# A third raw-weight buffer, loads in the order of use, and decoding and decay work moved, in a one-core state-space and expert kernel

## The chip, the cores and the metric

One core of one Trainium2 chip runs the whole program. The metric is the device time of one execution in microseconds (us); lower is better. Five engines work side by side, each through its own queue strictly in order: PE (TensorE, matrix products), ACT (ScalarE), DVE (VectorE), POOL (GpSimd) and SP, which here only issues transfers. An instruction whose operand or buffer is not ready holds up everything behind it on its engine.

## The reference

Three stages follow one another on 3072 tokens (4 sequences of 768) with 256 channels. Inputs are 32-bit floats; the three weights of stage two arrive as 64-bit floats.

```python
# stage 1: 8 heads, state 16 x 32, chunked along the sequence
cum = cumsum(log(a)); L = exp(cum[i] - cum[j]) for j <= i
y = (C B^T * L) x + (C state) * exp(cum)
state = exp(sum(log a)) * state + sum_j B_j x_j exp(cum_last - cum_j)
# stage 2
x = ((y @ w_a) * (y @ w_b)) @ w_out          # 256 -> 1536 -> 256
# stage 3: eight experts, the best of eight for each token
out[t] = gate * sigmoid * relu(x[t] @ w1[e]) @ w2[e]
```

## The kernel before, in words

**Tiles and stages.** The tokens are 24 tiles of 128, numbered `t`; tiles are prepared in units of two (`G = 2`). Stage two works on blocks of tiles (`BLK`, two tiles each for the first four blocks) and on 12 slices `f` of the 1536 inner columns (`NF1 = 12`). The code calls a slice's weights a unit as well; here they are "weights `f`". Every product of stage two is done as three float32r products of high and low halves (`mm3`, L513: `hi*hi`, `hi*lo`, `lo*hi`).

**One tile of stage one** (`attn_stages`): `tr` transposes B, Cq and cp on PE (`ptr`, L339) and ACT copies them out (`cd` L343, `BT` L345); `cb` multiplies them on PE (`pcb`, L365) and DVE multiplies by the decay mask (`mt`, L369); `ys` makes the output on PE (`py`, L386 to L396), ACT takes its high half (`xh`, L402), DVE its low half (`xl`, L403), and DVE updates the running state (`stm` L407, `Sst` L411). `pcb` of a tile needs the PSUM bank that `py` of the tile before used, so it waits for `xl` and `stm`. POOL prepares `cp`, `Cq`, `Bq` (L295) and the masks `lm` (L303) two tiles ahead (`prep`).

**Decays.** `decays(r)` computes the decay factors of half of all tiles (`r = 0` for tiles 0 to 11, `r = 1` for 12 to 23) in some 25 short DVE instructions (L213 to L252), eight PE transposes `pd` (L207), two or more ACT copies to `EX` (L208), one POOL product `dtmp` (L257) and one DVE sum `dec` (L264). The second group is queued when tile 7 is begun (`ahead(7)`), although tile 12 is the first to need it.

**Weights of stage two.** `load_w(f)` brings 768 KB of raw 64-bit weights into one of two `raw` buffers (`stg`, `bufs=2`; 256 KB each of `w_a`, `w_b`, `w_out`, L439 and L442). They are decoded to float32 halves in six pieces (`split_w`): ACT makes `u` (L464), DVE does `low3` (L468), `sign` (L472) and `join` (L476), ACT makes the high half `whi` (L480), DVE the low half `wlo` (L483). Weights 0 are decoded in three parts of 256 columns (`w_a`, `w_b`, `w_out`: lists `wa`, `wb`, `wo`), all others in one of 768. A raw buffer is free again after `sign`. `u` and `t` are work tiles of two buffers each.

**What sets the order.** The start of the program (tiles 0 and 1) is written out by hand, inside `tc.manual_schedule`, for PE, ACT, DVE and POOL. There the `wb` and `wo` parts and all of weights 1 (`w1_`) are decoded after tiles 0 and 1, in one run. From the barrier on, a scheduler orders the instructions, from a program in which `tick` after every product unit takes steps from three lists: attention steps (`pend`), background work (`bg`: `prep`, the second decays, loads of B and C) and decode pieces (`dq`, at `RATE`). SP issues the loads in program order.

Of the kernel before, what the change touches and what calls it, by code (L numbers as in the profile page):

```python
# [18 lines left out]
def kernel(  # L19
# [52 lines left out]
    stg = ctx.enter_context(tc.tile_pool(name="stg", bufs=2))  # L72
# [93 lines left out]
    def load_bc(u):  # L166

        v = wk.tile([P, 2, G, H, N], F32, tag="BCin", name="BCin")
        for j, src in ((1, B), (0, C)):
            for i in range(G):  # L170
                b, c = divmod(u * G + i, NCH)
                nc.sync.dma_start(
                    out=v[:, j, i], in_=src[b, :, c * P:(c + 1) * P, :].rearrange("h p n -> p h n"))
        BCin[u] = v
# [12 lines left out]
    rfs = cst.tile([NR, 2, P], F32, name="rfs")  # L187
# [5 lines left out]
    def decays(r):  # L193
# [5 lines left out]
        ar = araw[:, r, :]  # L199
        rf, rs = rfs[:, 0], rfs[:, 1]  # L200
        a0, T, A, Eb, t2, t3 = (small(n) for n in ("a0", "T", "A", "Eb", "t2", "t3"))
        bc = lambda t, n=SUB: t.unsqueeze(2).to_broadcast([NR, n, SP_])
# [37 lines left out]

        def ends():

            q = st["q"]
            V.tensor_copy(out=A, in_=a0)
            for i in range(SUB - 1):
                V.tensor_scalar(out=A[:, i + 1:], in0=A[:, i + 1:], scalar1=T[:, i:i + 1], scalar2=None, op0=ALU.mult)
            for i in range(1, SUB):
                V.tensor_scalar(out=Eb[:, 0:i], in0=Eb[:, 0:i], scalar1=T[:, i:i + 1], scalar2=None, op0=ALU.mult)
            V.tensor_tensor(out=sub(q[:, 1]), in0=sub(q[:, 0]), in1=bc(A), op=ALU.mult)
            V.tensor_tensor(out=sub(q[:, 2]), in0=sub(rs), in1=bc(Eb), op=ALU.mult)  # L250
            V.tensor_tensor(out=t3[:, 0:1], in0=T[:, 0:1], in1=Eb[:, 0:1], op=ALU.mult)
            V.tensor_copy(out=q[:, 3], in_=t3[:, 0:1].to_broadcast([NR, P]))  # L252
# [14 lines left out]
        return dict(new=new, factors=factors, pairs=pairs, ends=ends, tot=tot, tots=tots,  # L267
# [55 lines left out]
    def attn_stages(t):  # L323
# [51 lines left out]
        def ys(alt=False):  # L375
# [23 lines left out]
            if m not in xT:  # L399
# [45 lines left out]
    def split_w(f):  # L445
# [7 lines left out]
        def wide_pieces(s):  # L453
# [417 lines left out]
    def load_first2():  # L871
        for f0, n, tag in ((0, 3, "w64b"), (3, 3, "w64b"), (6, 2, "w64v")):
            r = wk.tile([P, n, DM], F32, tag=tag, name="raw2")
# [17 lines left out]
    with tc.manual_schedule(engines={ET.Activation, ET.DVE, ET.Pool, ET.PE}):  # L891
        load_a(0)
        load_bc(0)
        consts_early()
        load_x(0)
        load_w(0)
        load_x(1)
        load_bc(1)
        load_w(1)
        load_x(2)  # L900
        load_x(3)
        load_a(1)
# [4 lines left out]
        done = {"x": 4, "bc": 2}  # L907
# [4 lines left out]
        dq = []  # L912
        late_, first = [], []
        for f in range(NF1 + 1):
            ps = split_w(f) if f < NF1 else []
            if f < 2:
                first.append(ps)
                ps = []
            dq.extend(late_[:1] + ps[:1] + late_[1:])
            late_ = ps[1:]  # L920
            if f + 2 < NF1:
                late_.append(lambda f=f: load_w(f + 2))
# [8 lines left out]

        def ahead(t):
# [579 lines left out]
```

## Time and profile before

| | |
|---|---|
| median of three timed runs | 622.99 us (621.7 to 623.39) |
| the profiled execution | 621.96 us, of which span 620.3 us |
| PE busy | 569.3 us (92% of the span) |
| DVE busy | 325.5 us (52%) |
| ACT, POOL busy | 243.8 us (39%), 248.4 us (40%) |
| mean granted PE clock | 0.981 |

The span runs from the first to the last instruction of the profiled execution; its own time is 1.66 us longer. Busy time says how long an engine had an instruction in work, not that it was at its peak. The page of the profile cuts the span into 40 slices of 15.5 us and gives each engine's busy share in tenths. The other views list single instructions with their start, their duration and, in brackets, the idle time before them with the event that ended it. Matrix products overlap in the pipeline: the distance from one start to the next is what one of them costs.

### The profile page before, as it was taken

What the parts mean: (1) busy time and instruction counts of PE and PEld (TensorE: products, weight loads), DVE (VectorE), ACT (ScalarE), POOL (GpSimd) and SP (SyncE); (2) the same over time, 40 slices, a digit from 0 to 9 for tenths busy, and PEclk for the clock granted to TensorE, in tenths of its full rate; (3) what the DMA queues carried; (4) which work ended last, traced back from release to release, by engine and by line L of the source; (5) the groups of instructions that cost most, each with busy time, mean ns of one, the idle gap of its engine ahead of it and who ended that gap; (6) DMA issues with size and microseconds to landing.
All of it is one profiled execution on the core that took longest, in us unless ns stands there. A gap on an engine that the chain in (4) does not pass through costs nothing. (4 is left out here: it accounts for less than half of the span.)

```text
span 620.3 us, 11180 instructions
## 1 busy us (share of the span) xinstructions
PE 569.3 (92%) x4188; PEld 496.4 (80%) x4188; DVE 325.5 (52%) x894; ACT 243.8 (39%) x533; POOL 248.4 (40%) x319
## 2 busy tenths in 40 slices
PE   4369987999999999999999999999899999999991
PEld 2247867999897777777777889899788999999991
DVE  6779986224744434344232334544857556847620
ACT  3335553344333332332342233353345435445530
POOL 5547664333634433434222322364334433333111
PEclk9998997999999999999999999999999999999996
DMA  8597450002213210211000001221528345245000
GB/s 154 133 143 173 125 131 1 1 1 35 45 29 52 26 28 1 35 42 12 1 1 18 19 0 38 70 87 28 167 74 275 109 143 173 83 138 183 24 22 20
DMA packets 104920, 44.09 MB, mean 71 GB/s; under 512 B 81982, under 2 KB 99592, under 8 KB 104864
## 3 DMA queue, kind: packets, MB, share of 16 engines
q1 hardware_dynamic: 102128, 36.24, 23.7%
q0 software_dynamic: 2736, 7.12, 3.7%
q8 instruction: 34, 0.56, 0.4%
q14 instruction: 22, 0.18, 0.1%
HBM read 36.85 MB, written 6.95 MB: 71 GB/s over the span
## 5 line engine op out<-in xcount | busy, mean ns | idle before, releaser
L513 PE MATMUL pb<-xh,whi 128*128 128x256 f32 (+1 forms) x216 | 73.2, 339 | 1.7 <-ACT as__4671 L530 0.9
L513 PE MATMUL pa<-xh,whi 128*128 128x256 f32 (+1 forms) x216 | 72.0, 333 | 0.5 <-ACT xh L402 0.5
L513 PE MATMUL px<-gh,whi 128*128 128x256 f32 (+1 forms) x216 | 70.9, 328 | 0.0
L513 PE MATMUL pa<-xl,whi 128*128 128x256 f32 (+1 forms) x216 | 69.8, 323 | 0.0
L513 PE MATMUL px<-gl,whi 128*128 128x256 f32 (+1 forms) x216 | 69.2, 321 | 0.6 <-POOL gl L428 0.6
L513 PE MATMUL pa<-xh,wlo 128*128 128x256 f32 (+1 forms) x216 | 69.5, 322 | 0.0
L513 PE MATMUL px<-gh,wlo 128*128 128x256 f32 (+1 forms) x216 | 69.3, 321 | 0.0
L513 PE MATMUL pb<-xl,whi 128*128 128x256 f32 (+1 forms) x216 | 69.2, 320 | 0.0
L513 PE MATMUL pb<-xh,wlo 128*128 128x256 f32 (+1 forms) x216 | 69.1, 320 | 0.0
L1101 ACT ACTIVATE hh<-ph 128x384 fp32r<-128x384 f32 (+3 forms) x64 | 34.0, 531 | 69.7 <-PE ph L513 57.1
L1102 DVE SCALAR_TENSOR_TENSOR hl<-ph,hh 128x384 fp32r<-128x384 f32 (+3 forms) x64 | 38.7, 605 | 39.3 <-ACT hh L1101 33.8
L303 POOL TENSOR_SCALAR_AFFINE_SELECT lm<-EX 128x256 f32<-128x256 f32 x96 | 48.5, 541 | 24.2 <-DVE mt L369 22.6
L1121 PE MATMUL py<-eh,hh 128*128 128x256 f32 x200 | 57.0, 285 | 0.4 <-DVE hl L1102 0.4
L1121 PE MATMUL py<-el,hh 128*128 128x256 f32 x200 | 56.2, 281 | 0.0
L1121 PE MATMUL py<-eh,hl 128*128 128x256 f32 x200 | 56.1, 280 | 0.0
L1137 POOL DMA_INDIRECT out_dram<-yo,si x28 | 29.8, 1064 | 54.5 <-ACT yo L1134 47.7
L646 POOL DMA_INDIRECT xg<-x2d,gi x28 | 29.8, 1063 | 52.8 <-ACT lgx L661 36.9
L513 PEld LDWEIGHTS pb<-xh,whi 128*128 128x128 f32 x216 | 41.2, 191 | 10.7 <-issue 4.4
L513 PEld LDWEIGHTS pa<-xh,whi 128*128 128x128 f32 x216 | 41.3, 191 | 7.8 <-issue 3.7
L513 PEld LDWEIGHTS px<-gh,whi 128*128 128x128 f32 x216 | 41.0, 190 | 5.3 <-issue 2.1
L513 PEld LDWEIGHTS pa<-xh,wlo 128*128 128x128 f32 x216 | 41.4, 192 | 3.6 <-issue 0.3
L513 PEld LDWEIGHTS pa<-xl,whi 128*128 128x128 f32 x216 | 41.4, 192 | 3.3 <-issue 0.4
(685 smaller groups left out, 1402.3 us busy)
## 6 DMA issues: line engine op xcount, KB each, us to landing
raw<-in_moe_w_dram SPq DMA_DIRECT2D x30, 512.0 KB, 3.5
x2d<-xr SPq DMA_DIRECT2D x12, 272.0 KB, 2.2
xin<-in_x_dram SPq DMA_DIRECT2D x24, 128.0 KB, 2.9
raw<-in_moe_w_a_dram SPq DMA_DIRECT2D x12, 256.0 KB
raw<-in_moe_w_b_dram SPq DMA_DIRECT2D x12, 256.0 KB, 3.6
raw<-in_moe_w_out_dram SPq DMA_DIRECT2D x12, 256.0 KB, 4.1
BCin<-in_B_dram SPq DMA_DIRECT2D x26, 64.0 KB, 3.2
BCin<-in_C_dram SPq DMA_DIRECT2D x26, 64.0 KB, 3.1
```

Source lines behind the costliest of these rows:

```text
L303: nc.gpsimd.affine_select(out=Lm[t][:, :, s * SP_:(s + 1) * SP_], in_=exq(4 + s, b, c0 + i, 1).to_broadcast([P, H, SP_]), pattern=[[0, H], ...
L513: nc.tensor.matmul(out=out_, lhsT=l_, rhs=r_, start=first and i == 0, stop=last and i == 2, skip_group_check=skip)
L646: nc.gpsimd.indirect_dma_start(out=xg[:, q, :], out_offset=None, in_=x2d[0:nr, :], in_offset=bass.IndirectOffsetOnAxis(ap=sel["gi", i][:, ...
L1101: nc.scalar.activation(out=hh, in_=ph, func=AF.Relu)
L1102: V.scalar_tensor_tensor(out=hl, in0=ph, scalar=0.0, in1=hh.bitcast(F32), op0=ALU.max, op1=ALU.subtract)
L1121: nc.tensor.matmul(out=po, lhsT=l_[:, s_], rhs=r_, start=(f == 0 and j == 0 and q % 2 == 0), stop=(f == NF2 - 1 and j == 2), skip_group_ch ...
L1137: ins = nc.gpsimd.indirect_dma_start(out=out, out_offset=bass.IndirectOffsetOnAxis(ap=si[0:n_], axis=0), in_=yo, in_offset=None, bounds_ch ...
```

## The change

The raw weights get a third buffer (`stg`, `bufs=3`), and `load_w(2)` is issued at the start. The load of B and C is done tile by tile (`load_bc(u, i)`), and the first loads are issued in this order: B and C of tile 0, x of tile 0, B, C and x of tile 1, weights 0, weights 1, then B, C, x of tiles 2 and 3, weights 2. In the hand-written start four `wb` pieces stand before the `cb` of tile 1, the other two and the first `wo` piece before its `ys`. Weights 1 are no longer decoded in the start but stand in the list `dq` with the rest, and each further load follows its weights' pieces. The eight small products of `ends` (`A`, `Eb`, `all_`) become a step `parts`, which for the first group runs on POOL. The second group of decays is queued at tile 9, ahead of that tile's `prep`. `xl` comes after the state update. To make room, `u` of weights 0 to 5 uses the tiles `xr` and `x2T` in turn, `u` of weights 6 to 11 has one buffer in place of two, and `rfs` lies in the `cd` tiles.

```diff
-    stg = ctx.enter_context(tc.tile_pool(name="stg", bufs=2))
+    stg = ctx.enter_context(tc.tile_pool(name="stg", bufs=3))
...
+        def parts(g=None):
+            g = g or V
+            g.tensor_copy(out=A, in_=a0)
...
+            g.tensor_tensor(out=all_, in0=T[:, 0:1], in1=Eb[:, 0:1], op=ALU.mult)
...
             nc.scalar.activation(out=hi[:, :, i0:i0 + P], in_=py, func=AF.Copy)
-            nc.vector.tensor_tensor(out=lo[:, :, i0:i0 + P], in0=py,
-                                    in1=hi[:, :, i0:i0 + P].bitcast(F32), op=ALU.subtract)
             if c < NCH - 1:
...
+            nc.vector.tensor_tensor(out=lo[:, :, i0:i0 + P], in0=py,
+                                    in1=hi[:, :, i0:i0 + P].bitcast(F32), op=ALU.subtract)
...
-                    tl["u"] = wk.tile([P, 3 * DM], U32, tag="w64v", name="u", bufs=2)
+                    tag = ("xr", "x2T")[f % 2] if f < NE else "w64v"
+                    tl["u"] = wk.tile([P, 3 * DM], U32, tag=tag, name="u", bufs=1)
...
         load_a(0)
-        load_bc(0)
+        load_bc(0, 0)
         consts_early()
         load_x(0)
+        load_bc(0, 1)
+        load_x(1)
         load_w(0)
-        load_x(1)
-        load_bc(1)
         load_w(1)
+        load_bc(1, 0)
         load_x(2)
+        load_bc(1, 1)
         load_x(3)
+        load_w(2)
         load_a(1)
...
+        first = split_w(0)
+        dq = split_w(1) + [more_w]
...
-                if t == 7:
-
-                    d1 = decays(1)
-                    nop = lambda: None
-                    bg.extend([d1["new"], d1["factors"], d1["pairs"], d1["ends"], nop, nop, nop, nop,
-                               d1["ex"](0, 4), d1["ex"](4, 4), d1["tot"], d1["tots"]])
+                d1 = None
+                if t == 9:
+
+                    d1 = decays(1)
+                    bg.extend(d1[k_] for k_ in ("new", "factors", "pairs", "parts", "ends"))
...
         s0["tr"]()
+        dc["parts"](nc.gpsimd)
...
         dc["tot"]()
+        wb[0]()
+        wb[1]()
+        wb[2]()
+        wb[3]()
         s1["cb"]()
         s0["ys"](True)
         wa[5]()
+        wb[4]()
+        wb[5]()
+        wo[0]()
         dc["tots"]()
-        wb[0]()
         s1["ys"]()
-        for f_ in wb[1:] + wo:
+        for f_ in wo[1:]:
             f_()
         ahead(0)
         ahead(1)
-        bg.append(lambda: (load_bc(2), done.update(bc=3)))
-        bgstep()
-        for f_ in w1_:
-            f_()
-        bgstep()
-        dstep(2)
+        bg.append(more_bc)
+        bgstep(2)
         tc.no_sync_barrier()
```

How this moves instructions on two engines is shown at three places, in the order in which the built programs hold them. Line numbers differ by 3 to 4 between the two; the number behind a name is the buffer.

ACT, between the outputs of tile 1 (`xh`) and the copies of tile 2 (`cd`), before (`u_229` belongs to weights 0, `u_336` to weights 1, `u_407` to weights 2, `u_530` to weights 3):

```order
L402 ACTIVATE xh_289<-py_297 128x2x128
L480 ACTIVATE whi_107<-t_230 128x256
L464 ACTIVATE u_229<-raw_127 128x256
...
L464 ACTIVATE u_336<-raw_138 128x768
L480 ACTIVATE whi_107<-t_337 128x768
L464 ACTIVATE u_407<-raw_345 128x768
L530 ACTIVATE as__362<-pa_355 128x256
L464 ACTIVATE u_530<-raw_349 128x768
L343 ACTIVATE cd_389<-ptr_385,head2_81 128x128 x2
```

The same place in the changed program (`t_235` belongs to weights 0, `u_396` to weights 1, `u_544` to weights 2):

```order
L405 ACTIVATE xh_298<-py_308 128x2x128
L484 ACTIVATE whi_106<-t_235 128x256
L468 ACTIVATE u_396<-raw_132 128x768
L468 ACTIVATE u_544<-raw_145 128x768
L534 ACTIVATE as__351<-pa_344 128x256
L346 ACTIVATE cd_378<-ptr_374,head2_81 128x128 x2
```

Ahead of `cd` of tile 2 stood the rest of weights 0 (two `whi` and one `u`), all of ACT's part of weights 1, and `u` of weights 2 and 3. Now one `whi` of weights 0 stands there, and `u` of weights 1 and 2; `whi` of weights 1 and `u` of weights 3 come behind.

DVE, the last instructions ahead of the masks `mt` of tile 2, before (`t_337` is weights 1, `raw_345` and `t_408` weights 2, `raw_349` and `t_531` weights 3):

```order
L483 TENSOR_TENSOR wlo_108<-t_337,whi_107 128x768
L468 TENSOR_SCALAR raw_345<-raw_345 128x768
...
L472 SCALAR_TENSOR_TENSOR t_408<-raw_345 128x768
L468 TENSOR_SCALAR raw_349<-raw_349 128x768
L476 SCALAR_TENSOR_TENSOR t_408<-u_407,t_408 128x768
L472 SCALAR_TENSOR_TENSOR t_531<-raw_349 128x768
...
L483 TENSOR_TENSOR wlo_108<-t_408,whi_107 128x768
L369 TENSOR_TENSOR mt_396<-pcb2_398,lm_364 128x256
```

And in the changed program, from the output of tile 1 (`xl_299`) on (`raw_132` and `t_397` are weights 1, `raw_145` and `t_545` weights 2):

```order
L414 TENSOR_TENSOR xl_299<-py_308,xh_298 128x2x128
L472 TENSOR_SCALAR raw_128<-raw_128 128x256
L476 SCALAR_TENSOR_TENSOR t_235<-raw_128 128x256
L480 SCALAR_TENSOR_TENSOR t_235<-u_234,t_235 128x256
L487 TENSOR_TENSOR wlo_107<-t_235,whi_106 128x256
L472 TENSOR_SCALAR raw_132<-raw_132 128x768
L472 TENSOR_SCALAR raw_145<-raw_145 128x768
L476 SCALAR_TENSOR_TENSOR t_397<-raw_132 128x768
L476 SCALAR_TENSOR_TENSOR t_545<-raw_145 128x768
L480 SCALAR_TENSOR_TENSOR t_397<-u_396,t_397 128x768
```

Between tile 1's `xl` and tile 2's masks, which follow directly on this piece, there is now only the `w_out` part of weights 0, `low3` and `sign` of weights 1 and 2 and `join` of weights 1. Weights 1 and 2 were finished there before, and weights 3 begun; that work now stands behind the masks.

DVE around the updates of tile 7 (`xl`, `stm`), on which the second half of `pcb` of tile 8 waits, before:

```order
L540 TENSOR_TENSOR as__1050<-pb_1063,as__1050 128x256
L468 TENSOR_SCALAR raw_1414<-raw_1414 128x768
L483 TENSOR_TENSOR wlo_108<-t_1342,whi_107 128x768
L472 SCALAR_TENSOR_TENSOR t_1468<-raw_1414 128x768
L264 TENSOR_REDUCE dec_94<-dtmp_1115 128x12
L476 SCALAR_TENSOR_TENSOR t_1468<-u_1467,t_1468 128x768
L403 TENSOR_TENSOR xl_624<-py_1134,xh_623 128x2x128
```

The same place in the changed program:

```order
L472 TENSOR_SCALAR raw_1359<-raw_1359 128x768
L487 TENSOR_TENSOR wlo_107<-t_1287,whi_106 128x768
L544 TENSOR_TENSOR as__1045<-pb_1058,as__1045 128x256
L476 SCALAR_TENSOR_TENSOR t_1413<-raw_1359 128x768
L472 TENSOR_SCALAR raw_1464<-raw_1464 128x768
L408 TENSOR_TENSOR stm_1095<-py_1079,headh_80 128x128
L414 TENSOR_TENSOR xl_625<-py_1079,xh_624 128x2x128
```

The sum `dec` of the second decays is gone from here; it now stands behind the masks of tile 9. From the `pcb` of tile 8 on the order of PE is the same in both programs but for the eight `pd` transposes, which go from just ahead of tile 8's transposes to just ahead of tile 10's.

## Rows read from the trace of the kernel before

**Rows 1.** The page, span in 40 slices: PE busy, and PE's granted clock.

```profile
PE   4369987999999999999999999999899999999991
...
PEclk9998997999999999999999999999999999999996
```

**Rows 2.** Waits of PE: us in total, times, longest us.

```profile
PE pcb L365 <- ACT BT L345: 13.9, 3, 11.6
PE pcb L365 <- DVE stm L407: 4.6, 2, 3.8
```

**Rows 3.** Timeline of ACT, 20 to 35 us: start, duration, instruction [idle before].

```profile
23.03 0.42 ACT L480 ACTIVATE whi<-t 128x256 fp32r<-128x256 f32 x1 [2.71 <-DVE t L476]
...
30.18 0.37 ACT L530 ACTIVATE as__362<-pa 128x256 f32<-128x256 f32 x1
32.72 0.91 ACT L464 ACTIVATE u<-raw 128x768 f32<-128x768 f32 x1 [2.17 <-DMA raw<-in_moe_w_out_dram]
33.55 0.60 ACT L343 ACTIVATE cd<-ptr,head 128x128 f32<-128x128 f32 x2
```

**Rows 4.** Timeline of PE: the two long gaps, and products around 50 us.

```profile
34.48 1.24 PE L365 MATMUL pcb<-cd,BT 32*128 32x256 f32 x8 [11.56 <-ACT BT L345]
...
49.98 0.41 PE L513 MATMUL pa<-xl,whi 128*128 128x256 f32 x1
...
50.60 0.28 PE L513 MATMUL pb<-xh,wlo 128*128 128x256 f32 x1
...
96.19 1.22 PE L365 MATMUL pcb<-cd,BT 32*128 32x256 f32 x4 [3.84 <-DVE stm L407]
```

**Rows 5.** Timeline of POOL, 0 to 24 us.

```profile
1.88 0.20 POOL L132 TENSOR_TENSOR headh<-headm 128x4 f32<-128x4 f32 x1
2.16 0.19 POOL L134 TENSOR_TENSOR head<-headh 128x2 f32<-128x2 f32 x1
6.29 0.64 POOL L295 TENSOR_TENSOR cp<-BCin,EX 128x256 f32<-128x256 f32 x1 [3.94 <-DMA BCin<-in_C_dram]
8.59 4.02 POOL L303 TENSOR_SCALAR_AFFINE_SELECT lm<-EX 128x256 f32<-128x256 f32 x8 [1.65 <-ACT EX L208]
```

**Rows 6.** Timeline of SP, issue of the first x.

```profile
4.08 0.58 SPq L179 DMA_DIRECT2D xin<-in_x_dram  x1
```

**Rows 7.** Timeline of DVE, from tile 1's masks to tile 7's update.

```profile
15.61 1.35 DVE L369 TENSOR_TENSOR mt<-pcb,lm 128x256 f32<-128x256 f32 x3 [2.40 <-PE pyx L390]
...
21.55 0.53 DVE L468 TENSOR_SCALAR raw<-raw 128x256 uint32<-128x256 uint32 x1
...
36.06 1.35 DVE L369 TENSOR_TENSOR mt<-pcb,lm 128x256 f32<-128x256 f32 x3
...
51.39 0.42 DVE L540 TENSOR_TENSOR as__541<-pb,as__541 128x256 f32<-128x256 f32 x1
...
94.13 0.32 DVE L264 TENSOR_REDUCE dec<-dtmp 128x12 f32<-128x96 f32 x1 [2.94 <-POOL dtmp L257]
...
95.43 0.41 DVE L403 TENSOR_TENSOR xl<-py,xh 128x256 fp32r<-128x256 f32 x1
```

**Rows 8.** Busy time by stretch: PE, weight loads, DVE, ACT, POOL, granted clock, DMA.

```profile
51.39:95.43 44.04, 36.50 (x354) 31.34 (x353) 39.64 (x100) 24.50 (x58) 30.96 (x36) 0.99 0.55 132
...
101.50:445.00 343.50, 339.09 (x2504) 289.11 (x2503) 145.39 (x445) 126.60 (x297) 129.37 (x165) 1.00 0.15 33
...
50.37:96.19 45.82, 37.52 (x364) 32.26 (x362) 41.42 (x104) 25.97 (x60) 30.96 (x36) 0.98 0.55 130
96.19:101.50 5.31, 5.31 (x23) 4.66 (x24) 4.20 (x9) 0.61 (x2) 3.22 (x5) 0.50 0.00 0
```

**Rows 9.** Instructions touching tile q (second decays), 69 to 95 us: PE, weight loads, DVE.

```profile
69.00:95.00 26.00, 0.82 (x8) 0.75 (x8) 5.16 (x20) 0.99 0.43 105
```

**Rows 10.** Tile raw, 0 to 100 us: decode passes, ns min/median/max.

```profile
L468 DVE TENSOR_SCALAR raw<-raw x14: 281/552/811, 9.5 to 99.4; 128x768 uint32<-128x768 uint32 x11, 128x256 uint32<-128x256 uint32 x3
L472 DVE SCALAR_TENSOR_TENSOR t<-raw x13: 426/959/1500, 9.8 to 90.0; 128x768 uint32<-128x768 uint32 x10, 128x256 uint32<-128x256 uint32 x3
```

More of the change, by code (lines that the diff above doesn't have):

```diff
@@ L164, with load_bc @@
     xin, BCin = {}, {}
-    def load_bc(u):
-        v = wk.tile([P, 2, G, H, N], F32, tag="BCin", name="BCin")
+    def load_bc(u, i):
+        if i == 0:
+            BCin[u] = wk.tile([P, 2, G, H, N], F32, tag="BCin", name="BCin")
+        b, c = divmod(u * G + i, NCH)
         for j, src in ((1, B), (0, C)):
[L170 to L174, printed above, removed]
+            nc.sync.dma_start(out=BCin[u][:, j, i],
+                              in_=src[b, :, c * P:(c + 1) * P, :].rearrange("h p n -> p h n"))
     def load_x(t):
@@ L199, in decays @@
         ar = araw[:, r, :]
+        rfs = wk.tile([NR, 2, P], F32, tag="cd", name="rfs")
         rf, rs = rfs[:, 0], rfs[:, 1]
         a0, T, A, Eb, t2, t3 = (small(n) for n in ("a0", "T", "A", "Eb", "t2", "t3"))
+        all_ = cst.tile([NR, 1], F32, name=f"all{r}")
         bc = lambda t, n=SUB: t.unsqueeze(2).to_broadcast([NR, n, SP_])
@@ L239, in pairs @@
                                         scalar2=None, op0=ALU.mult)
+        def parts(g=None):
+            g = g or V
+            g.tensor_copy(out=A, in_=a0)
+            for i in range(SUB - 1):
+                g.tensor_scalar(out=A[:, i + 1:], in0=A[:, i + 1:], scalar1=T[:, i:i + 1], scalar2=None, op0=ALU.mult)
+            for i in range(1, SUB):
+                g.tensor_scalar(out=Eb[:, 0:i], in0=Eb[:, 0:i], scalar1=T[:, i:i + 1], scalar2=None, op0=ALU.mult)
+            g.tensor_tensor(out=all_, in0=T[:, 0:1], in1=Eb[:, 0:1], op=ALU.mult)
         def ends():
             q = st["q"]
[L244 to L248, printed above, removed]
             V.tensor_tensor(out=sub(q[:, 1]), in0=sub(q[:, 0]), in1=bc(A), op=ALU.mult)
             V.tensor_tensor(out=sub(q[:, 2]), in0=sub(rs), in1=bc(Eb), op=ALU.mult)
-            V.tensor_tensor(out=t3[:, 0:1], in0=T[:, 0:1], in1=Eb[:, 0:1], op=ALU.mult)
-            V.tensor_copy(out=q[:, 3], in_=t3[:, 0:1].to_broadcast([NR, P]))
+            V.tensor_copy(out=q[:, 3], in_=all_.to_broadcast([NR, P]))
         def tot():
@@ L265, in tots @@
                             in_=st["tmp"].rearrange("p b h c -> p b c h"), axis=AX.X, op=ALU.add)
-        return dict(new=new, factors=factors, pairs=pairs, ends=ends, tot=tot, tots=tots,
+        return dict(new=new, factors=factors, pairs=pairs, parts=parts, ends=ends, tot=tot, tots=tots,
                     ex=lambda k0, n: lambda: to_ex(k0, n))
@@ L872, in load_first2 @@
         for f0, n, tag in ((0, 3, "w64b"), (3, 3, "w64b"), (6, 2, "w64v")):
-            r = wk.tile([P, n, DM], F32, tag=tag, name="raw2")
+            r = wk.tile([P, n, DM], F32, tag=tag, name="raw2", bufs=1 if tag == "w64v" else None)
             nc.sync.dma_start(out=r, in_=w2[bass.ds(expert(0), 1), f0 * P:(f0 + n) * P, :]
@@ L906, with more_w @@
                                   in_=src[k * P:(k + 1) * P, :])
-        done = {"x": 4, "bc": 2}
+        done = {"x": 4, "bc": 2, "w": 3}
         bg = []
         RATE = [1.2, 0.6, 0.3, 0.4, 0.8]
-        dq = []
-        late_, first = [], []
-        for f in range(NF1 + 1):
+        def more_w():
+            if done["w"] < NF1:
+                load_w(done["w"])
+                done["w"] += 1
+        first = split_w(0)
+        dq = split_w(1) + [more_w]
+        late_ = []
+        for f in range(2, NF1 + 1):
             ps = split_w(f) if f < NF1 else []
-            if f < 2:
-                first.append(ps)
-                ps = []
             dq.extend(late_[:1] + ps[:1] + late_[1:])
-            late_ = ps[1:]
-            if f + 2 < NF1:
-                late_.append(lambda f=f: load_w(f + 2))
+            late_ = ps[1:] + [more_w]
         due = [0.0]
@@ L930, in dstep, with more_bc @@
                 due[0] -= 1
+        def more_bc():
+            for i in range(G):
+                load_bc(done["bc"], i)
+            done["bc"] += 1
         def ahead(t):
@@ L994 @@
         s0, s1 = st[0], st[1]
-        (wa, wb, wo), w1_ = first
+        wa, wb, wo = first
         V = nc.vector
```

5 lines of the change are left out of this document (3 added, 2 removed).

## The prediction

> **What bounds the kernel now.** I read the page's slices first. PE is at 9 tenths from the fourth slice to the last but one, except for a dip in the sixth and seventh; only the first seven slices, to about 108 us, leave it much idle, and there its clock dips too [rows 1]. So what this change can win lies before 108 us. From 101.5 to 445 us PE is busy 339.1 of 343.5 us [rows 8], and the order of instructions behind tile 8 is nearly the same: whatever PE gains by then is kept, whatever it loses is lost.
>
> The waits of PE name two large places, `pcb` on ACT's `BT` and `pcb` on DVE's `stm` [rows 2]; the timeline puts them at 34.48 us (11.56 us idle) and 96.19 us (3.84 us idle) [rows 4]. In the first, ACT tells why: `cd` of tile 2 stands behind the rest of weights 0, all of weights 1 and `u` of weights 2 and 3, and the last `u` waits 2.17 us for its raw weights to land [rows 3]. PE thus sits idle while decoding is done that its next products don't need. In the second, DVE waits 2.94 us for POOL's `dtmp` to make `dec`, with `xl` and `stm` queued behind it [rows 7]; no tile before 12 needs that sum.
>
> Two more things are to be seen. From 51.39 to 95.43 us DVE is busy 39.64 of 44.04 us against PE's 36.50 [rows 8]: there DVE, in its strict order, sets the pace. And PE runs at two levels: a product of 256 columns is listed with 0.41 us just before 50.2 us and 0.28 behind it [rows 4]; after the second gap the granted clock is 0.50 until 101.5 us [rows 8], 1.2 in place of 2.4 GHz.
>
> **The change, part by part.**
>
> *Loads and the first tile.* `cp` began at 6.29 us, on the landing of C [rows 5]. One more load, x of tile 0, now goes before that: at least its issue, 0.58 us [rows 6], at most about twice that if its transfer takes as long again. I take 0.8. The eight small products on POOL start every 0.28 us like two neighbours there [rows 5]: 2.2 us, into a hole of 1.65 us, the rest also within the 0.8. DVE is rid of them, but waits for POOL's result in the same hole: nothing. The swap of `xl` and the state update brings tile 1 forward by one `xl` at most, 0.41 us [rows 7]; I take half. Net, DVE is done with tile 1 at 21.6 us, as before (there `low3` began at 21.55 [rows 7]); bounds 21.2 to 22.4. The `wb` pieces now fill the 2.40 us in which DVE waited before tile 1's masks [rows 7] and the wait behind them: nothing, or some 2 us of DVE's time if that cover fails. B and C of tiles 2 and 3 now come behind weights 1 on SP's queue and land later by that transfer; the wait for ACT, until 26 us, covers POOL's work on them, and without it tile 2's transposes would wait for `Cq`.
>
> *The first gap.* For the `wo` part, `low3` to `whi` took 23.03 - 21.55 = 1.5 us, `whi` 0.42 [rows 3, 7]: ACT is at 23.5. Two `u` at 0.91, `as_` 0.37, then `cd` to `pcb`, 34.48 - 33.55 = 0.93 [rows 3, 4]: `pcb` at 26.6 us in place of 34.48, **7.9 us earlier**, if raw weights 2 have landed by 24.4; with the third buffer their load is issued without waiting for a release.
>
> *What is late next: DVE up to the product of slice 1 (51.39 us before [rows 7]).* From 21.6: `wo` 1.5 + 0.42 + 0.42; two `low3` at 0.55, two `sign` and one `join` at 0.96 (all passes of that size I take like `sign` [rows 10]) make 4.0: the masks of tile 2 start at 28.0 instead of 36.06 [rows 7]. Then come three masks of 1.35 us, two `wlo`, one `join` of weights 2, `sign` and `join` of weights 3 at 0.96, one `low3`, one product of 0.42, two tile updates (three instructions each, none over 0.41, so 1.0 together) and a constant: 4.05 + 4.8 + 0.55 + 0.42 + 2.0 + 0.2 = 12.0, so 40.0 without waits. I add 1.4 us, an estimate, for waits on `pcb`: 41.4 us, **10.0 us earlier**.
>
> *The DVE stretch, 51.39 to tile 7's `xl` (95.43).* Busy 39.64 [rows 8]. Out go the second decays: those touching q are 5.16 us [rows 9], with the short ones beside them about 6; they come back around tiles 8 to 10, where PE is the bound. Out goes a part of a mask, half of 1.35. In come four decode passes which were done in the gap before, 2 x 0.55 + 2 x 0.96 = 3.0, and about 0.9 of constants. That is 36.8 us; the 4.4 us idle of before I keep, though 2.94 of them were the wait for `dtmp`, since the weights are now decoded with less lead. End: 41.4 + 36.8 + 4.4 = 82.6. For more collisions with POOL I add 1.6: 84.2, **11.2 us earlier**. PE needs 37.52 us for its part of the stretch, less 0.82 for `pd` [rows 8, 9], which now falls under tile 10: it is not what decides.
>
> *The second gap and the clock.* `dec` is out of the way, so its 3.84 us are in that difference already. Behind it PE did 5.31 us of work at 0.50 [rows 8]; at the upper level that is 2.65 less.
>
> *Nothing elsewhere.* `u` of later weights has one buffer, but its next `u` stands just ahead of the `whi` that waits for the same `join`. Expert loads get the third buffer too; PE has little to gain from them behind 445 us.
>
> **Sum.** 11.2 + 2.65 = 13.9 us. The profiled execution took 621.96 us (span 620.3 and 1.7 around it), 1.0 below the median of the runs, 622.99: 608.1 by its own time, **609 us** against the median.
>
> **The rivals.**
>
> *Less: DVE gives most of it back.* Packing the same POOL and DVE work into fewer microseconds makes more passes collide: `sign` takes 0.96 in the middle and 1.50 at worst [rows 10]. From tile 2's masks on some 25 passes of that kind remain; if half of them lose 0.54 us more than in the sum, 6.8 us are gone: 616 us. Against it: half of the stretch collided before too. The Trainium skill ("SBUF — State Buffer", Who interferes with whom) says that a DVE instruction with two SBUF inputs and a GpSimd instruction that reads SBUF block each other. By that rule, moving `parts` to POOL and narrowing the stretch bring this case on; the spread between middle and worst agrees with it.
>
> *More: no waits.* Without the 1.4, 4.4 and 1.6 us of waits and collisions DVE's stretch ends at 76.8 us, just where PE ends with 40.0 + 36.7: 7.4 us more gain, 601.6 us.
>
> *The change doesn't do what it says.* If raw weights 2 land after 34 us, ACT's second `u` holds `cd` as long as before; then only the second gap goes, 3.84 + 2.65 = 6.5 us: 616.5 us. Against it: raw weights 2 follow 14 loads issued in one run, and there are some 4 us in hand.
>
> *Slower: PE stays at the lower level.* Up to 50 us PE, idle again and again, ran at 0.41 us a product [rows 4]. In the new stretch it has 36.7 us of work in about 43 and waits on DVE in many small pieces. Each microsecond of that work done at the lower level costs one more; 6 us are in hand beside DVE, 13.9 are won, so from 20 us of it on the change loses. At 25 us it is 5 us slower, 628. For it: gaps are spread, not gathered; against it: from 50.37 to 96.19 us PE was idle 8.3 us and its mean clock 0.98 [rows 8]. The Trainium skill ("TensorE: Matmul & The Clock Gate", A second HAM failure mode) tells of a kernel whose short idles between groups of products made the clock swing between both levels. By that rule this rival is the one to fear; the stretch before does not bear it out.
>
> **How the numbers follow.** The forecast (604 to 613): 0.60. Less gain, 613 to 619: 0.16. Weights late, 616: 0.07. More, under 604: 0.08. Gains and losses cancel: 0.04. Slower: 0.05. A difference of 0.3% (1.9 us) is about what a measurement of this kernel can tell from none: faster 0.91, the same 0.04, slower 0.05. The range of 603 to 617 holds the forecast, most of the two smaller gains and the edge of the larger, about 0.83; below and above it some 0.17 is left out.
>
> **What would show it.** Right: `pcb` of tile 2 near 26 to 28 us with no wait on `BT` over 4 us, and ACT's `u` not waiting for raw weights there; tile 2's masks near 28; the product of slice 1 near 41; `stm` of tile 7 near 82 to 86 with no `dec` ahead of it; no clock of 0.50 between 80 and 105 us; from there on the same rows some 14 us earlier. Wrong: a long wait of PE on DVE masks or on POOL's `gl` between 28 and 80 us, passes on DVE above 1.2 us throughout, the lower level beyond 60 us, or a new wait between 130 and 160 us when the decays come back.

## The result, and the profile after

| | before | after |
|---|---|---|
| median of 15 runs each, side by side | 623.42 us (619.18 to 627.66) | 618.87 us (616.12 to 622.0) |
| ratio after to before | | 0.9908, 95% interval 0.9884 to 0.9932 |
| span of the profiled execution | 620.3 us | 615.5 us |
| PE busy, mean granted clock | 569.3 us, 0.981 | 572.7 us, 0.985 |
| DVE busy | 325.5 us | 331.1 us |

The kernel is faster, by 4.6 us where 14 were forecast; 618.87 us lies above the range of 603 to 617. In two later comparisons it was 0.9876 (0.9856 to 0.9896) and 0.9916 (0.9886 to 0.9947): 4 to 8 us in all. One execution of the kernel with the second gap alone (below) took 650.92 us at a granted clock of 0.847; it is left out of that kernel's numbers.

The page of after, PE and its granted clock in 40 slices of 15.4 us, answers to [rows 1]:

```profile
PE   2689989999999999999999999999799999999991
...
PEclk9999989999999999999999999999979999999997
```

The dip of the sixth and seventh slice is nearly gone, the start still takes three slices, and a lower clock is new near the 30th slice. PE's timeline, to be held against [rows 4]:

```profile
29.54 1.24 PE L368 MATMUL pcb<-cd,BT 32*128 32x256 f32 x8 [2.33 <-ACT BT L348]
...
37.47 0.58 PE L517 MATMUL px<-gl,whi 128*128 128x256 f32 x1 [0.95 <-POOL gl L431]
...
45.12 0.38 PE L517 MATMUL pa<-xh,whi 128*128 128x256 f32 x1
45.35 0.28 PE L517 MATMUL pa<-xl,whi 128*128 128x256 f32 x1
...
87.89 0.71 PE L368 MATMUL pcb<-cd,BT 32*128 32x256 f32 x6 [1.14 <-DVE xl L414]
```

Both gaps are nearly closed: 11.56 us became 2.33, 3.84 became 1.14. But `pcb` of tile 2 comes at 29.54 us, not at 26.6. DVE, to be held against [rows 7]:

```profile
9.24 0.34 DVE L253 TENSOR_TENSOR q<-q,A 96x128 f32<-96x128 f32 x1 [2.84 <-POOL A L246]
10.29 0.29 DVE L254 TENSOR_TENSOR q<-rfs,Eb 96x128 f32<-96x128 f32 x1 [0.71 <-POOL Eb L248]
10.66 3.22 DVE L255 COPY q<-all 96x128 f32<-96x128 f32 x1
...
24.67 0.41 DVE L414 TENSOR_TENSOR xl<-py,xh 128x256 fp32r<-128x256 f32 x1
...
32.21 1.34 DVE L372 TENSOR_TENSOR mt<-pcb,lm 128x512 f32<-128x512 f32 x3
...
39.33 0.76 DVE L372 TENSOR_TENSOR mt<-pcb,lm 128x256 f32<-128x256 f32 x2 [1.76 <-PE pcb L368]
...
47.98 0.42 DVE L544 TENSOR_TENSOR as__528<-pb,as__528 128x256 f32<-128x256 f32 x1
...
87.33 0.41 DVE L414 TENSOR_TENSOR xl<-py,xh 128x256 fp32r<-128x256 f32 x1
```

One copy of 96 x 128 takes 3.22 us, where the same copy took 0.45 before. Tile 1's `xl` comes 4.3 us later than before, the product of slice 1 (`as__528`) 3.4 us earlier. The copy and tile 1's `xl` in the kernel before:

```profile
9.18 0.45 DVE L252 COPY q<-t 96x128 f32<-96x128 f32 x1
...
20.36 0.42 DVE L403 TENSOR_TENSOR xl<-py,xh 128x256 fp32r<-128x256 f32 x1 [2.10 <-ACT xh L402]
```

POOL in the same stretch of after, to be held against [rows 5]:

```profile
7.26 0.64 POOL L298 TENSOR_TENSOR cp<-BCin,EX 128x256 f32<-128x256 f32 x1 [4.90 <-DMA BCin<-in_C_dram]
...
10.58 3.22 POOL L306 TENSOR_SCALAR_AFFINE_SELECT lm<-EX 128x256 f32<-128x256 f32 x8
...
17.30 0.64 POOL L298 TENSOR_TENSOR cp<-BCin,EX 128x256 f32<-128x256 f32 x1 [2.03 <-DMA BCin<-in_C_dram]
```

POOL's eight masks and DVE's copy begin and end together. Last, busy time by stretch, columns as in [rows 8]:

```profile
47.98:87.33 39.35, 35.12 (x339) 29.98 (x337) 39.19 (x83) 23.76 (x56) 24.95 (x27) 1.00 0.64 152
88.60:92.15 3.55, 3.55 (x17) 3.55 (x18) 3.55 (x7) 1.95 (x3) 0.51 (x1) 0.52 0.00 0
446.00:454.00 8.00, 8.00 (x45) 8.00 (x45) 2.10 (x11) 0.69 (x2) 0.00 (x0) 0.57 0.01 2
```

From slice 1 to tile 7 DVE is now busy without a hole. PE runs at the lower level for 3.5 us behind the second gap (5.3 before) and for some 7 us from 447 us on, where the clock was 1.00 before. PE's lead over the kernel before, at the same instructions (times are those of after): 4.9 us at `pcb` of tile 2, 8.3 at `pcb` of tile 8, 9.3 at 135 us, 8.1 to 8.2 from 160 to 437 us, 5.0 at 456 us and 4.8 at the end.

### The profile page after: what moved, and what is told of

Same layout as the page of the kernel before. It is cut to its first block, busy times and chain, and to the rows that moved or that the text cites. A ratio compares the mean times of both kernels' runs of the same rounds, so it can differ in the third digit from the quotient of the medians.

```text
span 615.5 us, 11171 instructions
## 1 busy us (share of the span) xinstructions
PE 572.7 (93%) x4188; PEld 498.5 (81%) x4188; DVE 331.1 (54%) x886; ACT 243.1 (39%) x533; POOL 250.7 (41%) x327
## 5 line engine op out<-in xcount | busy, mean ns | idle before, releaser
L306 POOL TENSOR_SCALAR_AFFINE_SELECT lm<-EX 128x256 f32<-128x256 f32 x96 | 47.2, 527 | 9.9 <-DVE mt L372 9.9
L517 PEld LDWEIGHTS px<-gh,wlo 128*128 128x128 f32 x216 | 41.0, 190 | 4.6 <-issue 1.3
L517 PEld LDWEIGHTS px<-gl,whi 128*128 128x128 f32 x216 | 41.1, 190 | 4.1 <-POOL gl L431 1.2
```

The lines of the kernel that those rows point to most:

```text
L306: nc.gpsimd.affine_select(out=Lm[t][:, :, s * SP_:(s + 1) * SP_], in_=exq(4 + s, b, c0 + i, 1).to_broadcast([P, H, SP_]), pattern=[[0, H], ...
L517: nc.tensor.matmul(out=out_, lhsT=l_, rhs=r_, start=first and i == 0, stop=last and i == 2, skip_group_check=skip)
```

## The experiments

Three things were open: the locked copy, the missing time between tile 2's masks and slice 1, and the clock at the end. Each diff is against the kernel named. All ratios are against the kernel before, run in the same comparison, with 95% intervals.

**The changed kernel, twice more.** No edit.

> The changed kernel once more, nothing edited; its own time beside the other runs of this group, and a second look at TensorE's clock. In the first profile PE had nearly the same gaps at the change to the experts as before (0.70 us of work from 444 to 446 us), but behind them the granted clock was 0.50 from about 447.5 to 454 us, where it stayed at 1.00 before; 3.1 us were lost there. If that drop is chance, it is not there in every profile of this kernel or of the others with the same end, and PE's lead over the kernel before stays near 8 us to the end wherever it is missing. If the change brings it about, it is there again at the same place, 6 to 7 us long. Time 616 to 622 us either way.

> The changed kernel a third time, nothing edited, beside the two others of this group. Its time against the kernel before was 0.9908 in the first comparison and 0.9876 in the second, some 4.6 and 7.5 us; a third comparison tells which is the usual. Expected 0.986 to 0.992. The product of slice 1 lies at 48 to 50.4 us as in the first two profiles (forecast 41.4), and the granted clock behind tile 8 and at the change to the experts shows whether the two drops of the first profile come back: none in the second.

Measured 613.42 us (0.9876), below the 616 to 622 expected, and 619.84 us (0.9916, 0.9886 to 0.9947). The product of slice 1 came at 50.36 and 50.15 us. The lower level behind tile 8 is in neither profile; that at the change to the experts is in the third one and not in the second (second, then third):

```profile
440.00:454.00 14.00, 13.83 (x113) 13.26 (x112) 7.91 (x22) 6.95 (x13) 4.95 (x5) 1.00 0.16 44
```

```profile
448.00:460.00 12.00, 11.07 (x55) 11.07 (x56) 3.14 (x12) 1.66 (x5) 0.00 (x0) 0.57 0.05 13
```

It goes with one wait: in twelve of the seventeen profiles of this study PE waited 0.2 us there for ACT's `xB`, and none of them has the drop; in five it waited 1.3 us, and four of these have it (after and the third, and two kernels below), the fifth, that of the kernel before, not. So that loss, 3.1 us in the first profile, is not part of what the change does each time. Why the wait has two lengths was not tried.

**Parts back on DVE.**

```diff
-        dc["parts"](nc.gpsimd)
+        dc["parts"]()
```

> The eight small products (parts) of the first decays back on DVE, all else as in the changed kernel. Theory 'copy behind the burst': DVE's broadcast copy to q took 3.22 us because it fell together with POOL's eight lm instructions; with parts on DVE the copy comes before that burst, takes under 0.6 us, DVE's Cq starts near 12 us (14.98 in the changed kernel), tile 1's masks near 17 (19.68), and since DVE sets the pace up to tile 8 the 3 us are kept: pcb of tile 8 ends its wait near 85 us (87.89), total about 3 us below the changed kernel. Rival 'the start is hidden': the stretch to tile 8 is paced by loads and POOL, the 3 us are given back as waits, pcb of tile 8 stays at 87 to 88 us and the time within 1 us of the changed kernel.

Measured 611.4 us, 0.9832 (0.981 to 0.9854), 2.0 us below the changed kernel's 613.42 beside it. The copy took 0.21 us, tile 1's masks came at 16.25 us, and `pcb` of tile 2 at 26.38, where the forecast had it. But little of the 3 us reached tile 8 (`pcb` at 88.57 us, where the three profiles of the changed kernel have 87.89, 89.52 and 90.92; some 85 were expected). PE waited anew, and POOL shows why:

```profile
26.38 1.24 PE L368 MATMUL pcb<-cd,BT 32*128 32x256 f32 x8 [2.35 <-ACT BT L348]
...
36.24 0.58 PE L517 MATMUL px<-gl,whi 128*128 128x256 f32 x1 [3.09 <-POOL gl L431]
```

```profile
17.62 0.64 POOL L298 TENSOR_TENSOR cp<-BCin,EX 128x256 f32<-128x256 f32 x1 [4.07 <-DMA BCin<-in_C_dram]
...
21.38 7.83 POOL L306 TENSOR_SCALAR_AFFINE_SELECT lm<-EX 128x256 f32<-128x256 f32 x11
...
35.47 0.71 POOL L431 TENSOR_TENSOR gl<-as__351,gh 128x256 fp32r<-128x256 f32 x1
```

`gl` of slice 0 stands in POOL's queue behind the preparation of tiles 2 to 5, which began 4.1 us later than before, and `pcb` of tile 3 stands behind `px<-gl` on PE. From there to 49.70 us PE is busy 13.46 of 13.46 us at 0.21 us a product, and DVE waits for it: 5.5 us for `pcb`, 1.4 for the product of slice 1.

**The copy on ACT; two twins of the copy.** In the changed kernel, the first time ACT made the copy of `all_`; the second time two like copies, which need nothing from POOL, stood ahead of it on DVE.

```diff
-            V.tensor_copy(out=q[:, 3], in_=all_.to_broadcast([NR, P]))
+            if r == 0:
+                nc.scalar.activation(out=q[:, 3], in_=all_.to_broadcast([NR, P]), func=AF.Copy)
+            else:
+                V.tensor_copy(out=q[:, 3], in_=all_.to_broadcast([NR, P]))
```

```diff
+            if r == 0:
+                for _ in range(2):
+                    V.tensor_copy(out=ar, in_=T[:, 0:1].to_broadcast([NR, P]))
             V.tensor_copy(out=q[:, 3], in_=all_.to_broadcast([NR, P]))
```

> Parts stay on POOL; only the broadcast copy of all_ to q is made by ACT in place of DVE. Theory 'copy behind the burst': ACT's copy takes 0.2 to 0.4 us beside POOL's lm burst, pd of the second piece follows near 11.5 us, Cq on DVE starts at 12 to 13 us; of the 3.2 us some 2.5 come back, total 2 to 3 us below the changed kernel. Rival 'POOL's parts are late': the wait of DVE for A and Eb (2.84 and 0.71 us) is the cost, not the copy; then Cq starts after 14 us still, and the time is within 1 us of the changed kernel.

> Two more DVE copies of the same size and form (96x1 spread to 96x128) ahead of the copy of all_, which read T, made by DVE itself, and write a tile that is no longer read. Theory 'locked out': whichever copy starts first beside POOL's lm burst takes about 3 us until the burst ends, though it needs nothing from POOL; the copies behind it take 0.2 to 0.5 us. Rival 'late signal': the twins take 0.2 to 0.5 us each and only the copy of all_, which needs POOL's result, still ends at 13.8 us with the end of the burst.

Measured 613.52 us (0.9888, 0.9868 to 0.9909) and, in one run, 612.97 us: no gain. DVE and POOL of the first, then of the second:

```profile
10.48 3.79 DVE L475 TENSOR_SCALAR raw<-raw 128x256 uint32<-128x256 uint32 x1
...
10.57 3.23 POOL L309 TENSOR_SCALAR_AFFINE_SELECT lm<-EX 128x256 f32<-128x256 f32 x8
```

```profile
10.75 3.65 DVE L257 COPY araw<-T 96x128 f32<-96x128 f32 x2
14.32 0.21 DVE L258 COPY q<-all 96x128 f32<-96x128 f32 x1
...
10.84 3.23 POOL L309 TENSOR_SCALAR_AFFINE_SELECT lm<-EX 128x256 f32<-128x256 f32 x8
```

ACT's copy took 0.31 us, but now the next DVE instruction, a decode pass of 0.28 us, took 3.79. The twins took 3.65 together, the copy of `all_` behind them 0.21. So neither the copy nor POOL's signal was slow: with `parts` on POOL, whatever DVE started beside the first of that burst of eight masks (3.2 us) stood still to the end of the burst, in the first of the two for 0.5 us more. My expectation that ACT's copy would bring back 2.5 us was wrong for the same reason. The burst alone is not enough, though. In the kernel with all three edits (the last experiment), where `parts` are on DVE, the same copy began 0.03 us behind the first mask and took 0.22 us:

```profile
8.71 0.22 DVE L255 COPY q<-all 96x128 f32<-96x128 f32 x1
...
8.68 3.88 POOL L306 TENSOR_SCALAR_AFFINE_SELECT lm<-EX 128x256 f32<-128x256 f32 x8 [1.65 <-ACT EX L208]
```

All six profiles with `parts` on POOL have the block, and none of the eleven others; what in POOL's work ahead of the burst brings it about was not tried. The Trainium skill ("SBUF — State Buffer", Who interferes with whom) says that DVE and GpSimd share one pair of ports, and that beside a DVE instruction in a 2-port mode whoever issues first has the pair for its whole instruction, while the other blocks fully. Here DVE was blocked for eight instructions in a row, in these two kernels although its own is listed 0.09 us ahead of the first mask; in which mode it was, no run shows.

**Loads first.** With parts on DVE: B and C of tiles 2 and 3 ahead of weights 1; then also B and C of tile 1 ahead of the two x.

```diff
+        load_bc(1, 0)
+        load_bc(1, 1)
         load_w(1)
-        load_bc(1, 0)
         load_x(2)
-        load_bc(1, 1)
```

```diff
         load_bc(0, 0)
+        load_bc(0, 1)
         consts_early()
         load_x(0)
-        load_bc(0, 1)
         load_x(1)
```

> Parts on DVE as in the run before, and on top of that the four loads of B and C of tiles 2 and 3 ahead of weights 1 on SP's queue; the order on all other engines is the same. Theory 'POOL is late': with parts on DVE, pcb of tile 2 came at 26.4 us as forecast, but PE then waited 3.09 us for POOL's gl of slice 0 (35.47 us), which stands in POOL's queue behind the preparation of four tiles, and that began only at 17.62 us, after 4.07 us of waiting for C of tiles 2 and 3 (13.54 us in the kernel before). Now cp of tiles 2 and 3 starts at 13 to 14.5 us, gl at 32 to 33, PE's wait for it is under 0.7 us, pcb of tile 3 is at 33.5 to 34.5 (36.75 us), and the time falls by some 2 to 3 us. Rival 'weights late': weights 1 land later by the four transfers, ACT's u waits for them, pcb of tile 2 slips to 28 us or more and the time is the same or up to 2 us worse. Rival 'DVE takes it back': gl is early, but the stretch up to tile 8 is DVE's and ends at the same 88 to 89 us.

> The kernel of the run before this one, and the loads of x of tile 0 and 1 behind those of B and C of both tiles, as in the kernel before the change. Theory: cp of tiles 0 and 1 starts near 6.3 us in place of 7.3, and the whole chain of the first tiles comes forward by 0.9 us, pcb of tile 2 at 25.4; the time falls by up to 1 us. Rival: DVE's decays and ACT set the pace there, or what is won is lost up to tile 8: pcb of tile 2 within 0.3 us, no difference in the time.

Measured 610.18 us (0.982, 0.9795 to 0.9845) and 609.82 us (0.9815, 0.9788 to 0.9842): no difference that can be told from parts alone (0.9832), though `pcb` of tile 8 came at 87.30 and 86.28 us (88.57). POOL began tiles 2 and 3 at 13.7 us, but `gl` came at 33.5 only, since POOL then waited for B of tiles 4 and 5 with `gl` behind that; PE waited 1.75 and 2.92 us for it. The second kernel's POOL:

```profile
26.87 0.64 POOL L298 TENSOR_TENSOR Bq<-BCin,EX 128x256 f32<-128x256 f32 x1 [4.04 <-DMA BCin<-in_B_dram]
...
33.43 0.72 POOL L431 TENSOR_TENSOR gl<-as__351,gh 128x256 fp32r<-128x256 f32 x1
```

**The second gap alone.** In the kernel before, `dec` was queued at tile 9.

```diff
+        late_dec = []
...
+            if t == 9:
+                late_dec.pop()()
...
-                               d1["ex"](0, 4), d1["ex"](4, 4), d1["tot"], d1["tots"]])
+                               d1["ex"](0, 4), d1["ex"](4, 4), d1["tot"]])
+                    late_dec.append(d1["tots"])
```

> The kernel before the change, with one DVE instruction moved: the sum dec of the second decays, which waited 2.94 us for POOL's dtmp ahead of tile 7's update, is queued two tiles later. Nothing else of the change. Theory: PE's gap of 3.84 us before tile 8 and the granted clock of 0.50 behind it go, 6.5 us in all (bounds 3.8, if the clock falls all the same, and 6.5). Rival: what stands behind dec on DVE is late by itself, PE still waits 1.5 to 2.5 us there, and 1.5 to 3 us are won.

Measured 616.75 us (five executions) against 620.54, 0.9928 (0.9901 to 0.9955): 3.8 us in the medians. In its profile PE's lead went from -0.9 us at 84 us to 4.2 at 104, 5.1 us: PE no longer waits at that `pcb`, though its products ran at the lower level from 87 to 93 us. Of the term of 6.5 us the wait came and the clock at most in part: 3.8 to 5.1 us.

**Fillers on PE.** To the kernel with parts on DVE and the B and C loads first, 39 transposes that nobody reads were added where PE waited.

```diff
+    def warm(n):
+        pw = pp([P, P], name="pw")
+        for _ in range(n):
+            nc.tensor.transpose(out=pw, in_=ident, identity=ident)
```

> The kernel with parts on DVE and the loads of B and C first, with 39 transposes more on PE, whose result nobody reads, at four places where PE waited: 17 ahead of the first transposes, 5 ahead of pcb of tile 1, 6 ahead of its py, 11 ahead of pcb of tile 2. The order is otherwise the same. Theory 'idle keeps PE slow': up to 45 to 52 us in all runs a product of 256 columns followed another after 0.21 us, from there on after 0.12, and from 36 us on PE was busy without a gap, with DVE waiting for it 7.5 us; with PE kept busy the upper level comes 10 us earlier or more, the work from 26 to 50 us shrinks, and 3 to 6 us are won. Rival: the level does not follow from this idle time; the 0.12 us come at 45 to 52 us again and the time is the same or up to 1 us longer, by what the fillers delay. Rival 'DVE takes it back': the upper level comes early, but tile 8 starts at the same time, since DVE is busy throughout.

Measured 610.46 us (0.9823, 0.9797 to 0.985): the same. The upper level was there by 17 us (six fillers took 0.87 us from 16.79 us on, five took 1.27 from 12.90 on), so the early slow products do hang on PE's idle time, but it fell again behind PE's gaps, 0.54 on average from 26.6 to 41.4 us. A later kernel with 44 fillers and all three edits (below) also lost the level, from about 33 to 43 us, and was no better than without them: 609.47 us (0.9749, 0.9714 to 0.9784).

> The kernel of the run before with 44 fillers on PE (17, 6, 8 and 13) at the four places where PE waited before 26 us. In the run with 39 fillers the 0.12 us distance of products began at 21.3 us, but after gaps of 2.07 and 2.12 us at 23.4 and 31.5 us the granted clock fell to 0.50 from 26.7 to 41.5 us. With gl early one of the two gaps is gone. Theory: the lower level lasts shorter than in the run with 39 fillers, or does not come at all, and the time is 2 to 4 us below the run without fillers. Rival: one gap of some 1.6 us before pcb of tile 2 is enough, the level falls again to about 41 us, and the gain is under 1.5 us.

**`gl` of slice 0 on DVE.** One line, in three settings.

```diff
-        split(gh, gl, g, nc.gpsimd)
+        split(gh, gl, g, None if (m, f) == (0, 0) else nc.gpsimd)
```

The scheduler moves more with it: on PE `pcb` of tile 3, which stood behind `px<-gl`, goes ahead of it, and on ACT one `u` goes ahead of a `whi`. What the engine and what the order is worth can't be told apart here.

Alone, in the changed kernel; with parts on DVE (two edits), twice; with parts on DVE and both edits of the loads (all three), twice:

> The changed kernel with one edit: gl of slice 0 of the first block on DVE in place of POOL. Nothing else: parts on POOL, loads as in the change. It prices that one wait by itself. Theory 'the first gap stays open behind POOL': most of the forecast's missing time hangs on it, since PE's steady work, and with it the upper level of its clock, starts only behind px<-gl; the masks of tile 3 start at 35 to 37 us (39.3), the product of slice 1 at 42 to 46 (48 to 50.4), and the time is 4 to 8 us below the changed kernel, 0.975 to 0.983 of the kernel before. Rival 'all three together': DVE, late by the 3.2 us of the locked copy, is the bound there; the product of slice 1 moves by under 2 us and the time by under 2 us, and only with parts on DVE as well does the gain come.

> Parts and that gl on DVE, loads in the order of the change. Beside the run with all three edits (0.9745 of the kernel before; the product of slice 1 at 40.1 us) it tells what the order of the loads is worth. Theory: with gl off POOL's queue, POOL's late start on tiles 2 and 3 no longer holds anybody up, and only the 0.9 us of the first loads are lost: product of slice 1 at 41 to 42 us, the time 0 to 1.5 us above the run with all three, 0.974 to 0.978. Rival: the masks lm of tiles 3 and 4 come late from POOL and DVE waits for them, product of slice 1 at 44 us or later, 3 us or more lost.

> Parts and gl on DVE with the loads of the change, once more, beside the kernel with all three edits on the same chip: 0 to 1.5 us above it if the loads are worth only the 0.9 us of the first tiles; product of slice 1 at 45 to 46 us with the upper level at 45 us or later.

> On top of the early loads of B, C of all four first tiles and parts on DVE: gl of slice 0 of the first block is made by DVE in place of POOL, where it stood behind the preparation of tiles 4 and 5, which waits for its B and C until 25.6 to 26.9 us; PE then waited 1.75 to 3.09 us for gl at 34.2 to 36.2 us, and tile 3's pcb stands behind that product in PE's queue. PE's order differs only there (pcb of tile 3 goes ahead of px<-gl). Theory 'POOL's queue holds the first gap open': gl comes at 31 to 32 us, PE's wait goes, the masks of tile 3 start at 33 to 34 us (36.06), the product of slice 1 comes 1.5 to 2.5 us earlier than 46.93, and tile 8's pcb 1 to 2.5 us earlier than 86.28; the time falls by 1 to 2.5 us. Rival 'DVE takes it back': slice 1 comes earlier, tile 8 does not; the time is the same.

> The kernel with all three edits (parts on DVE, B and C of the first four tiles first, gl of slice 0 on DVE) once more, beside the one without the edit of the loads on the same chip. In its first profile PE came to the upper level at 32.4 us and the product of slice 1 at 40.12; all other kernels without fillers came to it at 45 to 54 us. Theory 'the level decides slice 1': if the level comes late this time, the product of slice 1 is at 44 to 45 us, like the kernel with two edits less the 0.9 us of the loads, and the time 0.976 to 0.979 of the kernel before; if it comes at 32 to 34 us again, 40 us and 0.973 to 0.976. Rival 'the loads decide': slice 1 is near 40 to 41 us whatever the level.

Measured: alone 611.79 us, 0.9846 (0.9822 to 0.987); two edits 608.55 us, 0.9798 (0.9771 to 0.9824), and 608.61 us, 0.9789 (0.9764 to 0.9814); all three 607.8 us, 0.9745 (0.9708 to 0.9782), and **603.17 us, 0.9721 (0.969 to 0.9752)**, 18.4 us below the kernel before. This beats both kernels. (The first profile of all three has the drop at the change to the experts, the second not.) PE of the kernel with all three (second profile), then of that with two edits beside it:

```profile
31.55 0.70 PE L368 MATMUL pcb<-cd,BT 32*128 32x256 f32 x4
32.18 0.39 PE L517 MATMUL px<-gl,whi 128*128 128x256 f32 x1
32.41 0.29 PE L517 MATMUL px<-gh,wlo 128*128 128x256 f32 x1
32.53 0.28 PE L517 MATMUL px<-gh,whi 128*128 128x256 f32 x1
```

```profile
46.56 0.38 PE L517 MATMUL pb<-xh,wlo 128*128 128x256 f32 x1
46.78 0.29 PE L517 MATMUL pb<-xh,whi 128*128 128x256 f32 x1
```

DVE of the kernel with all three: the masks of tile 2, the product of slice 1, `xl` of tile 7; and the stretch between the last two:

```profile
27.28 1.34 DVE L372 TENSOR_TENSOR mt<-pcb,lm 128x512 f32<-128x512 f32 x3
...
40.43 0.42 DVE L544 TENSOR_TENSOR as__528<-pb,as__528 128x256 f32<-128x256 f32 x1
...
78.94 0.41 DVE L414 TENSOR_TENSOR xl<-py,xh 128x256 fp32r<-128x256 f32 x1
```

```profile
40.43:78.94 38.51, 34.97 (x338) 29.84 (x336) 38.33 (x83) 23.94 (x56) 25.09 (x27) 1.00 0.62 151
```

`gl` alone takes PE's wait away but moves slice 1 hardly (49.03 us), and the time is 0.9846 of the kernel before, where the changed kernel had 0.9876 to 0.9916: 2 to 4 us, under the 4 to 8 expected, and 2 beside the second comparison (0.9876), whose profile like this one is without the drop at the change to the experts. With two edits the product of slice 1 came at 45.47 and 45.17 us, later than the 41 to 42 first expected. All three gain 4 to 6 us on the second kernel of the loads (0.9815), which lacks `gl` alone; 1 to 2.5 were expected.

Only with all three does PE come to its upper level at 31 to 32 us and keep it, in both profiles; with two edits it came at 49.2 and 46.8 us, though PE had worked almost without a gap from 29 us on (17.49 of 17.80 us to 46.8). The second kernel of the loads, with `gl` on POOL, had the level by 30.9 us (a first product of 0.39 us, 0.58 at the lower level) and lost it behind its wait for `gl`; the granted clock was 0.50 from 33.7 to 47.4 us:

```profile
30.90 0.39 PE L517 MATMUL px<-gh,whi 128*128 128x256 f32 x1
34.20 0.58 PE L517 MATMUL px<-gl,whi 128*128 128x256 f32 x1 [2.92 <-POOL gl L431]
```

So without fillers the early level came in the three profiles with both edits of the loads, and stayed where PE had no wait for `gl`. The loads, whose worth by themselves can't be told from none, are worth 5.4 us here in the medians (608.61 - 603.17) and 4.2 by the ratios; 0 to 1.5 were expected. Whether that is the level or the loads is not settled, since the level came early both times; nor is what in PE's work before 31 us brings it. With two edits PE waited 0.59 and 0.39 us for DVE's masks ahead of `py` of tile 2, and in those three profiles not at all; but it did not wait there either with the first edit of the loads alone, and was still at the lower level at 32 us.

## Why the prediction was wrong, and where it was right

The forecast's steps in us, beside what came:

| | forecast | after | parts on DVE | two edits | all three |
|---|---|---|---|---|---|
| DVE done with tile 1 | 21.6 | 25.1 | 21.9 | 21.6 | 21.1 |
| `pcb` of tile 2 | 26.6 | 29.5 | 26.4 | 26.1 | 25.6 |
| masks of tile 2 | 28.0 | 32.2 | 28.8 | 28.6 | 27.3 |
| product of slice 1 | 41.4 | 48.0 | 49.0 | 45.2 | 40.4 |
| `xl` of tile 7 | 84.2 | 87.3 | 88.0 | 84.4 | 78.9 |

(The two edits are shown by their second profile, all three likewise.)

*Wrong: "DVE is rid of them, but waits for POOL's result in the same hole: nothing."* With the small products on POOL, DVE reached its copy just as POOL's eight masks began, and stood for 3.22 us; tile 1 was done at 25.1 us, outside the bounds of 21.2 to 22.4. The eight products took POOL 2.7 us where 2.2 were forecast; the price was not theirs. With the products back on DVE the step came out at 21.9.

*Right: the first gap.* With that step mended, `pcb` of tile 2 came at 26.38 us against 26.6, with no wait of ACT for raw weights. The rival of the late weights is out.

*Wrong, and the larger error: "What is late next: DVE up to the product of slice 1".* The step summed DVE's passes, 12.0 us, and gave PE and POOL 1.4 us of waits. The step took 15.8 to 18.0 us from tile 2's masks on in the three profiles of the changed kernel, and 20.1 with the first step mended (28.8 to 49.0), where 13.4 were forecast. POOL's `gl` of slice 0 and PE at 0.21 us a product were the path there. Both could be seen ahead of the run: in PE's order in the changed program `pcb` of tile 3 stands behind `px<-gl` (in the kernel before it went ahead of it, 40.03 against 41.61 us), and PE's products took 0.41 until 50.2 us [rows 4]. I moved PE's work ten microseconds forward and priced it as if its level came with it. With all three edits the same step took 40.43 - 27.28 = 13.15 us against 13.4 forecast, so the sum of DVE's passes was sound; it was not what ended last.

*Wrong: the cover of the late B and C.* I had ACT cover them "until 26 us". ACT did, but `gl`, which stands behind them on POOL's queue, was wanted by PE from 33 us on (parts on DVE).

*Better than forecast: DVE's stretch to tile 7.* 39.35 us in after and 38.51 with all three, against 42.8: of the 4.4 us of idle that I kept 0.16 were left (39.35 - 39.19). The busy time was 39.19, near the 36.8 + 1.6 of the sum. This gave back some 3.5 us of the lost 6.6.

*The second gap* closed to 1.14 us as forecast, but the level fell once more in the first profile: 0.9 us of the clock's 2.65 came (all of it in the other two, where it stayed up). *The eight `pd` under tile 10*, which I moved there without a price, have 0.88 us of PE's busy time where PE is the bound; the lead fell by 0.7 us at that point. *The change to the experts* took 3.1 us in the profiled run by the clock, which the forecast did not have, and which the second profile does not have either.

The rivals of lost gain (616 us) and of late weights (616.5) were nearest in time, but by other causes: the first had DVE's passes collide one by one, and the loss was one block at 10.7 us and a queue; the second did not come, since ACT's `u` had no wait for raw weights ahead of tile 2. The rival of the lower level was right about the place (PE's products stayed at 0.41 up to 45 to 54 us in the three profiles of the changed kernel), wrong about the size. The Trainium skill ("TensorE: Matmul & The Clock Gate", A second HAM failure mode), which I had named there, tells of short idles that make the clock swing; the run with fillers agrees, with its level up by 17 us and down again behind a gap of 2.07 us before `pcb` of tile 2.

## What to carry to other kernels

When a wait is closed, list for every engine what stands in its queue between there and the next point that you price, and ask of each which of them ends last; a sum along the engine that was last before is only a lower bound. Work moved to POOL shifts what DVE starts beside POOL's next burst; here that cost DVE 3 us, more than the work itself, so move it where DVE has nothing due. And work of PE that is brought forward into its start may come at the level of the start: here at 0.21 us a product, not 0.12, until a trace of the changed kernel shows otherwise.

## What was not expected of the hardware

With `parts` on POOL the masks shut DVE out for a whole burst of eight (3.2 us, whichever instruction DVE had: 3.22, 3.79 and 3.65 us), while in the kernel before the same eight took 4.02 us [rows 5] with DVE's passes, 0.28 to 0.64 us each, between them. In the shut-out cases DVE's instruction began within 0.1 us of the burst's first mask. That does not decide it: with all three edits the same copy began 0.03 us behind the first mask and took 0.22 us. What does was not tried.

PE ran products 0.21 us apart for 13.5 us without a gap before it came to the upper level (parts on DVE, 36.2 to 49.7 us), and in that stretch the granted clock is listed as 1.00 all the same. There the distance of the products tells the level, not the clock's column.
